# Inverting the first two pairs of chunks side by side, with 14 weight conversions ahead of them: a recurrent attention and two MLPs on one Trainium2 core

## The chip, the core and the metric

The kernel runs on one core of one Trainium2 chip. The core has five engines that each take their own instructions in order: PE (matmuls and, through an identity, transposes), DVE (element by element work), ACT (copies, casts, activations and a DMA queue), POOL (element by element work and a DMA queue) and SP (a DMA queue only). They meet at semaphores. The transfers of all three queues run on 16 DMA engines. The metric is the device time of one execution in microseconds.

## What is computed

Three stages follow each other. First a recurrence over 768 time steps for 4 x 8 = 32 pairs of batch and head, each with a 40 x 40 state:

```python
for t in range(S):                      # B, H, S, D = 4, 8, 768, 40
    y[:, :, t] = np.einsum('bhd,bhde->bhe', rt, state)
    Sa = np.einsum('bhde,bhe->bhd', state, at)
    state_decay = state * wt[:, :, None, :] - np.einsum('bhd,bhe->bhde', Sa, bt)
    state = state_decay + np.einsum('bhd,bhe->bhde', vt, kt)
```

Its output, as x of 3072 tokens by 320, goes through an MLP with 2048 hidden units (`h = x @ w_in`, an ELU, `g @ w_out`), and that through a routed MLP: each token goes to the expert of 8 that its largest logit names (`relu(x @ w1[e]) @ w2[e]`, times the gate). All is in float32; `w_in` and `w_out` come as float64.

## The kernel before

**The recurrence in chunks.** The 768 steps are cut into 24 chunks of 32 (`C`), two chunks make a pair, and there are 12 pairs (`NP`). Four pieces of work serve a pair `p`:

- `lanes(g)`, once for two pairs: products of the decays `w` along the chunk, and `a`, `b`, `k` scaled by them, written to DRAM (`scr_A`, `scr_W`, `scr_BK`). Group 0 runs on DVE at the start, the later ones on POOL.
- `pre(p)`: loads the scaled rows into `tok` tiles, transposes them on PE (L253, PSUM tag "p", one bank), forms the products of a chunk (L288), masks them on DVE into `keep` (L294) and stores the part that has to be inverted in DRAM, as `Td[p]` (L299).
- `inverse(p)`: loads `Td[p]` (64 triangular matrices of 32 x 32) on SP into both halves of a tile (L315) and inverts them on DVE in 31 steps. A step is three instructions: a tensor product into `ut` (L323), an update of one column (L328, with a scalar for each partition) and an addition (L330). The tile `inv` holds input and result. The result goes to DRAM as `Ud[p]` (L334) and from there into the `UT` tiles of the two chunks (L339).
- `chain(c)`, once a chunk: X from v and the state (L398), its product with U (L383 on `X,UT`, evacuated into `pv`, L412 and L414), the state update on DVE (L428, L429), GN (L441), the output `xtok` (L456) and its transposes for the MLP. Chunk c + 1 needs chunk c's state.

**Weights.** `Moe1.weights` turns `w_in` and `w_out` from float64 into two float32r parts, in 40 conversions. One is fetched through ACT's queue into one of three `raw` tiles, goes through an absolute value on ACT (L515), four or five instructions on DVE (L516 to L519, L481) and a copy on ACT; those of `w_out` also have transposes (L556) and small matmuls (L560) on PE. `block(p)` is the first MLP for a pair, 16 hidden tiles each (L609, then L613 to L615, then L623 to L625), and needs the weights and the outputs of both chunks.

**Order.** A scheduler puts the instructions of all engines in order when the program is built. It follows the order in which the code is written, except that pieces in `ahead(tc, g, offset)` come forward by so many places. `tc.issue_after(ins)` queues what a block writes on the engine of `ins` behind `ins`. `weave` takes steps of several generators in turn. At the start `first` (lanes 0, `pre(0)`, `inverse(0)`, lanes 1) is woven with nine conversions, then `pre(1)` with the rest. In the loop over `p` the chain of pair `p`, `inverse(p + 1)`, `pre(p + 2)`, a part of lanes and `block(p - 1)` are woven.

Of the kernel before, what the change touches and what calls it, by code (L numbers as in the profile page):

```python
# [10 lines left out]
F32 = mybir.dt.float32  # L11
# [6 lines left out]
ALU = mybir.AluOpType  # L18
# [20 lines left out]
class Attention:  # L39
# [31 lines left out]
    def setup(self, ident, psum):  # L71
# [52 lines left out]
        self.loaded = self.taken = self.banks = 0  # L124

    def lanes(self, g, eng, eng2=None, room=None):
# [53 lines left out]
        ps = self.psum("p")  # L180
# [39 lines left out]
    def load_tok(self):  # L220
# [3 lines left out]
        kind, i = self.order[self.loaded]  # L224
        t = self.t("tok", self.loaded)
# [82 lines left out]
    def inverse(self, p):  # L308
# [27 lines left out]
        for cc in range(2):  # L336
            for b in range(4):
                h = 32 * cc + 8 * b
                self.returned = self.nc.sync.dma_start(  # L339
                    self.t("UT", 2 * p + cc)[32 * b:32 * b + 32], self.Ud[p][:, h:h + 8, :])  # L340
        yield

# [28 lines left out]
    def chain(self, c, put):  # L371
# [88 lines left out]
        if c + 2 < NCH:  # L460
            self.load_pv(c + 2)
        nc.scalar.copy(xt[:, 320:384], xt[:, 256:320])
# [21 lines left out]
class Moe1:  # L484
# [81 lines left out]
    def begin_x(self, ctx, i):  # L566
        pool = ctx.enter_context(self.tc.tile_pool(name=f"moe1_x{i}", bufs=1))
        self.xH.append(pool.tile([128, 3, 256], F32R, name=f"xH{i}"))
        self.xL.append(pool.tile([128, 3, 256], F32R, name=f"xL{i}"))
# [471 lines left out]
def drain(g):  # L1041
    for _ in g:
        pass
# [31 lines left out]
def body(ctx, tc, r, k, v, w, a, b, w_in, w_out, w_gate, w1, w2, out, capacity=768):  # L1075
# [27 lines left out]
    moe1.begin(st["moe1"], psum)  # L1103
    put = moe1.put_x(ident, psum)
    stage = ExitStack()
    pool = stage.enter_context(tc.tile_pool(name="stage", bufs=1))
# [11 lines left out]
    def start():  # L1118
        lanes = att.lanes(0, nc.vector, room=room)
        for _ in range(25):  # L1120
            next(lanes)
            yield
        pre = att.pre(0)
        drain(lanes)
        yield from pre
        inverse = att.inverse(0)
        next(inverse)
        with tc.issue_after(att.last.ins):
            att.load_pv(0)
            att.load_bkd(0)  # L1130
            att.load_wp(0)
            att.load_pv(1)
        yield
        drain(att.lanes(1, nc.gpsimd))
        yield from inverse
# [15 lines left out]
    weave((first, 20), (behind(att.scaled.ins, some(conv, 9)), 20))  # L1151
    weave((ahead(tc, att.pre(1), 1000), 10), (behind(att.inverted.ins, conv), 40))
    lanes = None
    for p in range(NP + 1):
        gens = []
        if p < NP:
# [3 lines left out]
            if p + 1 < NP:  # L1160
                gens.append((ahead(tc, att.inverse(p + 1), 1500), 20))
# [3 lines left out]
        if p == 1:  # L1165
            stage.close()
            moe1.begin_x(stage, 2)
# [75 lines left out]
```

## Time and profile before

| | |
|---|---|
| time, median of 3 runs | 1213.22 us (1212.05 to 1215.55) |
| time of the profiled execution | 1217.03 us |
| its span, first to last instruction | 1215.3 us |
| PE busy | 1027.2 us (85%) |
| DVE busy | 822.6 us (68%) |
| ACT busy | 599.1 us (49%) |
| POOL busy | 256.1 us (21%) |
| mean granted clock of PE | 0.904 of full speed |

A busy share is an average over stages with different limits; what a change in one stage is worth is read in that stage. Rows give a start in us from the span's beginning, a length in us, the engine and the line in the kernel's code. The profiled execution took 3.8 us more than the median.

### The profile page before, as it was taken

Reading aid. Unit: us, or ns where it says so; the run is one execution under the profiler, and the core shown is the slowest. Engines: PE = TensorE matmul, PEld = TensorE weight load, DVE = VectorE, ACT = ScalarE, POOL = GpSimd, SP = SyncE. Lnnn points to the kernel's source line nnn. Section 1 sums busy time; section 2 is a strip of 40 time slices with the busy share of each in tenths; the row PEclk is TensorE's granted clock in tenths of the full one; section 3 lists DMA queues with packets and bytes.
Section 4 is the critical chain, followed back from the end, with each engine's and each line's share of the span. In section 5 each row is a group of like instructions: output and inputs, shape, how many; then the busy total and the mean of one; then the engine's idle time right before and its main releaser. Section 6 shows DMA issues by size and latency. Waiting matters only on the chain.

```text
span 1215.3 us, 35896 instructions
## 1 busy us (share of the span) xinstructions
PE 1027.2 (85%) x14568; PEld 933.5 (77%) x14568; DVE 822.6 (68%) x2755; ACT 599.1 (49%) x1499; POOL 256.1 (21%) x314
## 2 busy tenths in 40 slices
PE   0454588888988989889999979999998798989995
PEld 0344478777976988779888879888988697979995
DVE  6676798998679576968596949686445456545541
ACT  1432246564654655556556655656655345434420
POOL 5355543410035100400000000000001232323311
PEclk9855669899998989899999989999989999989998
DMA  6887667663356544452616351522131165544210
GB/s 217 205 196 217 188 166 173 194 132 65 62 103 176 104 67 81 106 104 51 108 31 101 58 104 30 91 50 44 27 88 25 39 188 159 164 134 124 82 45 22
DMA packets 294400, 131.27 MB, mean 108 GB/s; under 512 B 261560, under 2 KB 276032, under 8 KB 294224
## 3 DMA queue, kind: packets, MB, share of 16 engines
q1 hardware_dynamic: 276672, 76.39, 32.2%
q0 software_dynamic: 10064, 37.39, 9.7%
q10 hardware_dynamic: 7488, 15.09, 4.1%
q8 instruction: 117, 1.92, 0.7%
q14 instruction: 59, 0.48, 0.1%
HBM read 99.13 MB, written 31.00 MB: 107 GB/s over the span
## 4 chain that ended last, share of the span: by engine, by line
PE 41%; DVE 27%; DMA 19%; ACT 5%; issue 5%; SPq 2%; POOL 1%; ACTq 0%; POOLq 0%; DVEq 0%
PE ps_h L609 8%; PE ps_c L383 4%; DVE inv L328 4%; DVE inv L330 4%; DVE ut L323 3%; DMA out_dram<-ys,ids 3%; DMA inv<-Td 3%; PE ps_o L623 3%; PE ps_o L625 3%; PE ps_o L624 3%; PE ps_c L931 2%; DMA Td<-keep 2%; PE ps_h L931 2%; DMA r<-in_moe_w_dram 2%; DMA Ud<-inv 2%
## 5 line engine op out<-in xcount | busy, mean ns | idle before, releaser
L480 ACT CAST gH<-e 128x256 fp32r<-128x256 f32 x192 | 77.2, 405 | 116.7 <-DVE e L615 102.0
L623 PE MATMUL ps_o<-woH,gH 128*128 128x328 f32 x384 | 129.5, 340 | 5.2 <-ACT gH L480 4.5
L728 POOL DMA_INDIRECT list<-ids,idx x24 | 24.1, 1004 | 498.4 <-DVE idx L724 306.8
L624 PE MATMUL ps_o<-woL,gH 128*128 128x328 f32 x384 | 125.7, 329 | 0.0
L625 PE MATMUL ps_o<-woH,gL 128*128 128x328 f32 x384 | 120.7, 336 | 4.9 <-DVE gL L481 4.8
L615 DVE SCALAR_TENSOR_TENSOR e<-e,ps_h 128x256 f32<-128x256 f32 x184 | 76.2, 415 | 69.0 <-ACT e L614 65.5
L609 PE MATMUL ps_h<-xH,wiH 128*128 128x256 f32 x368 | 113.0, 308 | 10.4 <-DVE e L615 6.6
L323 DVE TENSOR_TENSOR ut<-inv 128x30 f32<-128x30 f32 (+4 forms) x360 | 93.2, 259 | 29.0 <-DMA inv<-Td 28.6
L609 PE MATMUL ps_h<-xL,wiH 128*128 128x256 f32 x368 | 108.6, 295 | 0.0
L609 PE MATMUL ps_h<-xH,wiL 128*128 128x256 f32 x368 | 108.5, 296 | 0.0
L328 DVE SCALAR_TENSOR_TENSOR inv<-inv 128x1 f32<-128x1 f32 (+15 forms) x372 | 101.5, 273 | 0.6
L330 DVE TENSOR_TENSOR inv<-inv,ut 128x30 f32<-128x30 f32 (+4 forms) x360 | 99.7, 277 | 0.2
L481 DVE TENSOR_TENSOR gL<-e,gH 128x256 fp32r<-128x256 f32 x192 | 81.3, 426 | 26.7 <-ACT gH L480 23.3
L253 PE MATMUL ps_p<-ident,tok 128*104 128x128 f32 x288 | 55.0, 320 | 49.4 <-DMA tok<-scr_A 24.8
L613 ACT ACTIVATE e<-ps_h 128x256 f32<-128x256 f32 x184 | 70.3, 384 | 53.4 <-PE ps_h L609 33.9
L609 PEld LDWEIGHTS ps_h<-xH,wiH 128*128 128x128 f32 x368 | 73.7, 201 | 15.0 <-DVE e L615 9.5
L623 PEld LDWEIGHTS ps_o<-woH,gH 128*128 128x128 f32 x384 | 76.8, 200 | 7.7 <-ACT gH L480 5.5
L614 ACT ACTIVATE e<-e 128x256 f32<-128x256 f32 x192 | 79.1, 417 | 4.3
L625 PEld LDWEIGHTS ps_o<-woH,gL 128*128 128x128 f32 x384 | 73.6, 199 | 7.9 <-DVE gL L481 7.2
L253 PEld LDWEIGHTS ps_p<-ident,tok 128*104 128x104 f32 x288 | 35.9, 148 | 56.4 <-issue 25.5
L624 PEld LDWEIGHTS ps_o<-woL,gH 128*128 128x128 f32 x384 | 77.1, 201 | 0.5
L609 PEld LDWEIGHTS ps_h<-xL,wiH 128*128 128x128 f32 x368 | 74.1, 201 | 0.1
(323 smaller groups left out, 2867.5 us busy)
## 6 DMA issues: line engine op xcount, KB each, us to landing
r<-in_moe_w_dram SPq DMA_DIRECT2D x15, 640.0 KB
tok<-scr_BK SPq DMA_DIRECT2D x48, 160.0 KB
BKd<-scr_BK SPq DMA_DIRECT2D x48, 160.0 KB
r<-in_moe_w_dram SPq DMA_DIRECT2D x7, 1024.0 KB
W<-in_w_dram POOLq DMA_DIRECT2D x10, 640.0 KB, 6.3
scr_BK<-lx POOLq DMA_DIRECT2D x10, 640.0 KB, 3.5
inv<-Td SPq DMA_DIRECT2D x24, 256.0 KB
raw<-in_moe_w_out_dram ACTq DMA_DIRECT2D x16, 320.0 KB
```

What stands on the lines that cost most here:

```text
L253: self.nc.tensor.transpose(ps[0:104, 128 * j:128 * j + 128], t[:, 2 * q:2 * q + 2, :].rearrange("p a e -> p (a e)")[:, 0:104], self.ident,)
L323: nc.vector.tensor_tensor(tv, TL[:, j:j + 1, j + 2:32].to_broadcast([128, n, m]), UL[:, 0:n, j:j + 1].to_broadcast([128, n, m]), ALU.mult,)
L328: nc.vector.scalar_tensor_tensor(col, UL[:, 0:n, j], TL[:, j, j + 1:j + 2], col, ALU.mult, ALU.add)
L330: self.inverted = nc.vector.tensor_tensor(UL[:, 0:n, j + 2:32], UL[:, 0:n, j + 2:32], tv, ALU.add)
L480: split.last = nc.scalar.copy(H, x)
L481: return (low or nc.vector).tensor_tensor(L, x, H.bitcast(F32), ALU.subtract)
L609: nc.tensor.matmul(h, l, r, start=i == 0, stop=i == len(seq) - 1)
L614: nc.scalar.activation(e, e, AF.Exp, scale=-1.0)
L615: nc.vector.scalar_tensor_tensor(e, e, -1.0, h, ALU.add, ALU.max)
L623: nc.tensor.matmul(o, gH[:, ts], self.woH[:, f], start=f == 0, stop=False)
L624: nc.tensor.matmul(o, gH[:, ts], self.woL[:, f], start=False, stop=False)
L625: nc.tensor.matmul(o, gL[:, ts], self.woH[:, f], start=False, stop=f == NF - 1)
```

## The change

Pairs 0 and 1 are no longer inverted one after the other. `pre(1)` is written ahead of the inverse, with the priority of `first`. A new `inverses` loads `Td[0]` and `Td[1]` into a tile `twice` of its own and does the 31 steps for both at once: the two tensor instructions of a step now have twice the elements, and the column update, whose scalar differs by pair, is written twice. The results of both pairs are stored, then U is loaded for chunks 0, 1 and 2; as there are three `UT` tiles, that for chunk 3 is loaded in chunk 0's chain, behind its `xtok`. The loop starts with `inverse(2)`, at `p` = 1.

Around it: 14 conversions instead of nine are woven with `first`, and the other 26 are written behind the joint inverse. One load of `tok` rows, ("a", 2), is held until the loads for the inverse and those behind it stand in SP's queue. The transposes of lanes 1 use PSUM tag "o". `stage` (the `raw` and `xf` tiles, later `xH2` and `xL2`) lies on the right side, and the MLP's working tiles are opened when `twice` is given back.

```diff
         self.loaded = self.taken = self.banks = 0
+        self.hold = True
 
...
-        ps = self.psum("p")
+        ps = self.psum("o" if g == 1 else "p")
...
         kind, i = self.order[self.loaded]
+        if self.hold and (kind, i) == ("a", 2):
+            return
...
         for cc in range(2):
-            for b in range(4):
-                h = 32 * cc + 8 * b
-                self.returned = self.nc.sync.dma_start(
-                    self.t("UT", 2 * p + cc)[32 * b:32 * b + 32], self.Ud[p][:, h:h + 8, :])
-        yield
+            self.load_ut(p, cc)
+        yield
+
+    def inverses(self, room):
+
+        nc = self.nc
+        TL = room.rearrange("p (q a b) -> p q a b", q=2, a=32)
+        UL = self.inv[:, 0:1024].rearrange("p (q a b) -> p q a b", q=2, a=16)
+        ut = [self.inv[:, 1024 + 256 * i:1280 + 256 * i] for i in range(2)]
+        nc.vector.memset(self.inv[:, 0:1024], 0.0)
+        for i in range(2):
+            half = slice(64 * i, 64 * i + 64)
+            for q in range(2):
+                self.last = self.nc.sync.dma_start(TL[half, q], self.Td[q])
+                nc.vector.memset(self.inv[half, 512 * q:512 * q + 512][:, i::34], 1.0)
+        yield
+        for j in range(31):
+            n, m = j // 2 + 1, 30 - j
+            if m:
+                tv = ut[j % 2][:, 0:2 * n * m].rearrange("p (q a b) -> p q a b", q=2, a=n)
+                nc.vector.tensor_tensor(
+                    tv, TL[:, :, j:j + 1, j + 2:32].to_broadcast([128, 2, n, m]),
+                    UL[:, :, 0:n, j:j + 1].to_broadcast([128, 2, n, m]), ALU.mult,
+                )
+            for q in range(2):
+                col = UL[:, q, 0:n, j + 1]
+                nc.vector.scalar_tensor_tensor(
+                    col, UL[:, q, 0:n, j], TL[:, q, j, j + 1:j + 2], col, ALU.mult, ALU.add)
+            if m:
+                rest = UL[:, :, 0:n, j + 2:32]
+                self.inverted = nc.vector.tensor_tensor(rest, rest, tv, ALU.add)
+            if j % 2 == 1:
+                yield
+        for p in range(2):
+            for i in range(2):
+                self.nc.sync.dma_start(
+                    self.Ud[p].rearrange("(a i) l t -> i l a t", i=2)[i], UL[64 * i:64 * i + 64, p])
+            for cc in range(2 - p):
+                self.load_ut(p, cc)
+        yield
+
+    def load_ut(self, p, cc):
+        for b in range(4):
+            h = 32 * cc + 8 * b
+            self.returned = self.nc.sync.dma_start(
+                self.t("UT", 2 * p + cc)[32 * b:32 * b + 32], self.Ud[p][:, h:h + 8, :])
...
+        if c == 0:
+            self.load_ut(1, 1)
...
     moe2 = Moe2(tc, nc, w1, w2, out, route, ident)
     moe1.begin_x(st["moe1"], 0)
     moe1.begin_x(st["moe1"], 1)
-    moe1.begin(st["moe1"], psum)
+    moe1.psum = psum
     put = moe1.put_x(ident, psum)
     stage = ExitStack()
-    pool = stage.enter_context(tc.tile_pool(name="stage", bufs=1))
+    pool = stage.enter_context(tc.tile_pool(name="stage", bufs=1, side="right"))
+    beside = ExitStack()
+    twice = beside.enter_context(tc.tile_pool(name="beside", bufs=1)).tile([128, 2048], F32, name="twice")
...
     conv = moe1.weights(pool, route)
         pre = att.pre(0)
         drain(lanes)
         yield from pre
-        inverse = att.inverse(0)
+        yield from att.pre(1)
+        inverse = att.inverses(twice)
         next(inverse)
         with tc.issue_after(att.last.ins):
             att.load_pv(0)
             att.load_bkd(0)
             att.load_wp(0)
             att.load_pv(1)
-        yield
-        drain(att.lanes(1, nc.gpsimd))
+            drain(att.lanes(1, nc.gpsimd))
+            att.hold = False
+            att.load_tok()
+        yield
         yield from inverse
...
 
     with tc.issue_after(att.landed.ins):
         next(conv)
-    weave((first, 20), (behind(att.scaled.ins, some(conv, 9)), 20))
-    weave((ahead(tc, att.pre(1), 1000), 10), (behind(att.inverted.ins, conv), 40))
+    weave((first, 26), (behind(att.scaled.ins, some(conv, 14)), 20))
+    drain(behind(att.inverted.ins, conv))
+    beside.close()
+    moe1.begin(st["moe1"], psum)
     lanes = None
...
             gens.append((ahead(tc, chained(att.chain(2 * p, put), att.chain(2 * p + 1, put)), 2000), 32))
             if p % 2 == 0:
                 lanes = att.lanes(p // 2 + 2, nc.gpsimd) if p // 2 + 2 < NP // 2 else iter(())
-            if p + 1 < NP:
+            if p > 0 and p + 1 < NP:
                 gens.append((ahead(tc, att.inverse(p + 1), 1500), 20))
             if p + 2 < NP:
                 gens.append((ahead(tc, att.pre(p + 2), 1500), 20, 6))
             gens.append((ahead(tc, some(lanes, 14) if p % 2 == 0 else lanes, 500 if p == 0 else 2000), 14))
         if p == 1:
             stage.close()
-            moe1.begin_x(stage, 2)
+            moe1.begin_x(stage, 2, side="right")
```

In the built programs the lines of the changed kernel are numbered otherwise: L294 became L297, L323 to L330 became L360 to L370 for the joint inverse (L326 to L333 for the later ones), L339 became L384, L428 and L429 became L472 and L473, L456 became L500, L516 to L519 became L562 to L565.

On DVE, at the entry of the first inverse. Before, it begins right behind the second mask of pair 0 (`keep`, L294) and the copies of lanes 1 (`WCT`):

```order
L481 TENSOR_TENSOR woL<-x_565,woH 128x320
L294 TENSOR_TENSOR keep<-ps_p,m_tm_131 128x512
L184 COPY WCT_147<-ps_p 40x64
L185 COPY WCT_147<-ps_p 40x64
L481 TENSOR_TENSOR woL<-ps_r,woH 128x8
L323 TENSOR_TENSOR ut_179<-inv 128x30
L328 SCALAR_TENSOR_TENSOR inv<-inv 128x1
L330 TENSOR_TENSOR inv<-inv,ut_179 128x30
```

In the changed kernel the joint inverse begins behind the fourth mask, the second of pair 1, and behind the 14th conversion, whose last instructions stand around that mask:

```order
L565 SCALAR_TENSOR_TENSOR xf<-raw,xf 128x320
L159 MEMSET W_143 128x40
L297 TENSOR_TENSOR keep<-ps_p,m_tm_131 128x512
L527 TENSOR_TENSOR woL<-xf,woH 128x320
L527 TENSOR_TENSOR woL<-ps_r,woH 128x8
L360 TENSOR_TENSOR inv<-twice,inv 128x60
L366 SCALAR_TENSOR_TENSOR inv<-inv,twice 128x1
L370 TENSOR_TENSOR inv<-inv 128x2x30
```

So the inverse moved behind two more masks and five more conversions.

On SP, the queue of loads and stores around the first inverse. Before, the load for pair 0's inverse (`inv<-Td0`) stands behind the second store of `Td0`, and the loads of v, BKd and Wp for chunk 0 follow it; `Td1` comes later:

```order
L299 DMA Td0_107<-keep_166 32x16x32 x2
L315 DMA inv_178<-Td0_107 64x1024 x2
L213 DMA pv0_151<-in_v_dram 32x16x40 x2
L349 DMA BKd0_175<-scr_BK0_101 64x16x40 x2
L354 DMA Wp0_176<-scr_W0_95 32x8x40 x4
L213 DMA pv1_152<-in_v_dram 32x16x40 x2
L239 DMA tok1_150<-scr_BK0_101 64x16x40 x2
L213 DMA tok0_149<-in_r_dram 64x16x40 x2
L299 DMA Td1_108<-keep_166 32x16x32 x2
```

In the changed kernel both stores of `Td1` and the load of it stand ahead of chunk 0's v, BKd and Wp:

```order
L302 DMA Td0_107<-keep_166 32x16x32 x2
L353 DMA twice_231<-Td0_107 64x1024 x2
L242 DMA tok1_150<-scr_BK0_101 64x16x40 x2
L214 DMA tok0_149<-in_r_dram 64x16x40 x2
L302 DMA Td1_108<-keep_166 32x16x32 x4
L353 DMA twice_231<-Td1_108 64x1024 x2
L214 DMA pv0_151<-in_v_dram 32x16x40 x2
L393 DMA BKd0_175<-scr_BK0_101 64x16x40 x2
L398 DMA Wp0_176<-scr_W0_95 32x8x40 x4
```

Chunk 0's loads moved behind pair 1's store and load, and the last rows of pair 1 ahead of all of them.

On DVE again, in chunk 0's state update (`ST`). Before, the first steps of pair 1's inverse stand between its two halves:

```order
L428 TENSOR_TENSOR ST_155<-ps_c,ST_155 40x8x40 x2
L516 SCALAR_TENSOR_TENSOR x_789<-x_789,raw 128x256
L429 TENSOR_TENSOR ST_155<-ST_155,WCT_146 40x8x40 x2
L517 TENSOR_SCALAR raw<-x_789 128x256
L323 TENSOR_TENSOR ut_179<-inv 128x30
L328 SCALAR_TENSOR_TENSOR inv<-inv 128x1
L428 TENSOR_TENSOR ST_155<-ps_c,ST_155 40x8x40 x2
```

In the changed kernel only conversions are mixed in:

```order
L565 SCALAR_TENSOR_TENSOR x_963<-raw,x_963 128x256
L472 TENSOR_TENSOR ST_155<-ps_c,ST_155 40x8x40 x2
L473 TENSOR_TENSOR ST_155<-ST_155,WCT_146 40x8x40
L527 TENSOR_TENSOR wiL<-x_963,wiH 128x256
L473 TENSOR_TENSOR ST_155<-ST_155,WCT_146 40x8x40
L472 TENSOR_TENSOR ST_155<-ps_c,ST_155 40x8x40 x2
```

The inverse's steps are gone from there. Counted over DVE's whole order, 24 of the 40 conversions begin ahead of chunk 1's `xtok` before and 32 in the changed kernel. Ahead of chunk 5's `xtok` stand all 40 in both, with 31 hidden tiles of the first MLP before and 32 in the changed kernel, and the whole inverses of pairs 0 to 3 in both.

## Rows read from the trace of the kernel before

**Rows 1.** Busy time by stretch: stretch, length, engines' busy us, granted clock, DMA share, GB/s.
```profile
core 0: us, PE busy (x) PEld busy (x) DVE busy (x) ACT busy (x) POOL busy (x), PEclk, DMA share, GB/s
60.00:80.00 20.00, 10.05 (x62) 6.97 (x61) 11.15 (x40) 6.72 (x14) 11.14 (x14) 0.50 1.05 233
...
142.56:182.73 40.17, 31.78 (x541) 26.80 (x539) 34.67 (x103) 17.35 (x44) 17.53 (x25) 0.66 0.73 191
182.73:337.39 154.66, 136.44 (x2319) 121.61 (x2315) 130.63 (x446) 89.73 (x248) 30.98 (x35) 0.92 0.55 124
302.34:337.39 35.05, 35.05 (x606) 32.49 (x601) 22.79 (x78) 21.68 (x56) 0.00 (x0) 0.91 0.36 58
405.49:530.05 124.56, 114.59 (x2128) 103.39 (x2127) 94.50 (x361) 71.53 (x182) 15.76 (x13) 0.93 0.47 86
```

**Rows 2.** DVE in order of time, inverse of pair 0: start, length, instruction, idle before.
```profile
70.55 0.19 DVE L323 TENSOR_TENSOR ut<-inv 128x30 f32<-128x30 f32 x1 [5.38 <-DMA inv<-Td]
...
72.74 2.85 DVE L328 SCALAR_TENSOR_TENSOR inv<-inv 128x2 f32<-128x2 f32 x1
...
79.41 0.28 DVE L323 TENSOR_TENSOR ut<-inv 128x120 f32<-128x120 f32 x1
79.60 0.23 DVE L328 SCALAR_TENSOR_TENSOR inv<-inv 128x6 f32<-128x6 f32 x1
79.74 0.28 DVE L330 TENSOR_TENSOR inv<-inv,ut 128x120 f32<-128x120 f32 x1
...
91.05 0.19 DVE L323 TENSOR_TENSOR ut<-inv 128x30 f32<-128x30 f32 x1
...
92.86 0.24 DVE L328 SCALAR_TENSOR_TENSOR inv<-inv 128x16 f32<-128x16 f32 x1
```

**Rows 3.** The chain that ended last: stores and loads of Td, pairs 0 and 1.
```profile
61.49 3.79 DMA Td<-keep
...
65.86 4.66 DMA inv<-Td
...
106.94 8.99 DMA Td<-keep
...
116.50 8.85 DMA inv<-Td
```

**Rows 4.** PE in order of time: pair 1's last product, chunks 0 and 2.
```profile
86.35 0.69 PE L288 MATMUL ps_p<-Abd,BKT 104*64 104x64 f32 x8
...
104.30 0.31 PE L383 MATMUL ps_c<-X,UT 32*32 32x40 f32 x2 [6.87 <-DMA UT<-Ud]
...
191.91 0.79 PE L383 MATMUL ps_c<-pv,keep 32*32 32x40 f32 x64
...
207.70 0.76 PE L383 MATMUL ps_c<-X,UT 32*32 32x40 f32 x60
```

**Rows 5.** DVE in order of time: xtok of chunks 0, 1 and 5.
```profile
142.56 0.48 DVE L456 TENSOR_TENSOR xtok<-ps_c,Wp 128x320 f32<-128x320 f32 x1
...
182.73 0.49 DVE L456 TENSOR_TENSOR xtok<-ps_c,Wp 128x320 f32<-128x320 f32 x1
...
337.39 0.48 DVE L456 TENSOR_TENSOR xtok<-ps_c,Wp 128x320 f32<-128x320 f32 x1
```

**Rows 6.** DVE in order of time, chunk 0: two long waits, in square brackets.
```profile
112.36 0.49 DVE L516 SCALAR_TENSOR_TENSOR x<-x,raw 128x320 f32<-128x320 f32 x1 [3.07 <-ACT x L515]
...
125.45 0.48 DVE L323 TENSOR_TENSOR ut<-inv 128x30 f32<-128x30 f32 x1 [4.88 <-DMA inv<-Td]
```

**Rows 7.** DVE in order of time: the 1st, 9th, 24th and 40th conversion's first instruction.
```profile
22.31 0.42 DVE L516 SCALAR_TENSOR_TENSOR x<-x,raw 128x256 f32<-128x256 f32 x1
...
57.39 0.49 DVE L516 SCALAR_TENSOR_TENSOR x<-x,raw 128x320 f32<-128x320 f32 x1 [0.40 <-ACT x L515]
...
177.85 0.49 DVE L516 SCALAR_TENSOR_TENSOR x<-x,raw 128x320 f32<-128x320 f32 x1 [0.25 <-ACT x L515]
...
276.60 0.48 DVE L516 SCALAR_TENSOR_TENSOR xf<-xf,raw 128x320 f32<-128x320 f32 x1
```

**Rows 8.** Groups by line, PE, chunks 2 to 5 (182.73 to 337.39): count, busy us, mean ns.
```profile
L560 PE MATMUL ps_r<-wg,raw 128*128 128x8 f32 (+1 forms) x48 | 7.7, 269 | 0.3 <-ACT raw L558 0.3
```

More of the change, by code (lines that the diff above doesn't have):

```diff
@@ L564, in weights, with begin_x @@
                 yield
-    def begin_x(self, ctx, i):
-        pool = ctx.enter_context(self.tc.tile_pool(name=f"moe1_x{i}", bufs=1))
+    def begin_x(self, ctx, i, **kw):
+        pool = ctx.enter_context(self.tc.tile_pool(name=f"moe1_x{i}", bufs=1, **kw))
         self.xH.append(pool.tile([128, 3, 256], F32R, name=f"xH{i}"))
```

## The prediction, made before the changed kernel ran

> **What bounds the kernel now.** I read the busy shares by stretch first, then DVE's and PE's instructions in order of time from 20 to 410 us, then the chain that ended last where a transfer stands in it. The reader is to see that no engine is full early on: in 60 to 80 us PE is busy half the time at a granted clock of 0.50, the lower of its two levels, DVE 56%, and only the DMA engines are full (1.05) [rows 1]. The front is a chain of latencies: mask of the products, store and load of Td, the inverse on DVE, store and load of its result, then chunks 0 and 1. Later PE fills up: all 35.05 us of the sixth chunk, and 114.59 of 124.56 us (92%) in chunks 8 to 11 [rows 1]. So the change is worth what it does to the moment at which chunk 5 ends: in both orders all 40 conversions, 31 or 32 hidden tiles of the first MLP and the inverses of pairs 0 to 3 stand ahead of that point on DVE, and behind it the orders run alike. I call the write of xtok a chunk's end: chunk 0 at 142.56, chunk 1 at 182.73, chunk 5 at 337.39 [rows 5].
>
> **The change, step by step, on the clock of the profiled execution.** That one took 1217.03 us, 3.8 above the median of 1213.22; the difference found is carried over to the median.
>
> *The joint inverse starts later.* Before, pair 0's inverse starts at 70.55 [rows 2], behind a store of 3.79 and a load of 4.66 us [rows 3], and pair 1's front work runs under it. Now it needs pair 1's last mask. The product for that one ended on PE at 87.0 (86.35 + 0.69) [rows 4], with a transpose of r ahead of it; 86 for the end of the mask. Then follow an issue, the store, an issue and the load: 0.5 + 3.8 + 0.5 + 4.7 = 9.5 us as for pair 0, or 0.5 + 9.0 + 0.5 + 8.9 = 18.9 as for pair 1 [rows 3]. I take 11, near the lower, because pair 0's crossing came in a slice with full DMA engines and the loads of v, BKd and Wp that stood there now queue behind this one on SP. Start 97 (95 to 105).
>
> A rule speaks against that choice. The Trainium skill, page "DMA: Bandwidth & Descriptors", section "Issuing engines are not separate DMA queues", says that transfers from different engines run on the same 16 DMA engines and interleave: the raw weights of the five conversions moved ahead, 1.4 MB (256 or 320 KB each), would then hold Td back by an estimated 6 us at the slice's 233 GB/s. By it the sum would be 6 us worse; the upper end of 105 covers as much without it.
>
> *Its length.* 120 elements take 0.28 and 30 take 0.19 us: 1.0 ns each. A step is two such tensor operations and a column operation; the first two start 0.19 apart and the next follows after 0.14 (79.41, 79.60, 79.74) [rows 2], so a step with 120 elements is 0.19 + 0.14 + 0.19 = 0.52 us, 0.28 of it fixed. Over 31 steps a pair has 2600 elements in each of the two lines: 31 x 0.28 + 5.2 = 13.9 us, 27.8 for two pairs. Jointly the column operation is issued twice: 31 x (0.28 + 0.14) + 10.4 = 23.4 us. The inverse of pair 0 really ran to 93.1 (92.86 + 0.24) with stretches like the 2.85 us at 72.74 [rows 2], taken while POOL worked on 1280 elements; I leave one in: 26.3. End 123.3. Were there no fixed part, it would be 27.8, 4.4 more.
>
> *The way back.* From the inverse's end to chunk 0's product with U took 11.2 us (93.1 to 104.30) [rows 2, 4]; two more stores are issued ahead of the loads, at the 0.6 us or so that lies between a landing and the next transfer [rows 3]: +1.2. Chunk 0's product at 135.7, **31 us later**.
>
> *Chunk 0* took 38.3 us from there. DVE stood 3.07 us at a conversion's raw weights and 4.88 us at the load for pair 1's inverse, which was queued ahead of the second state update [rows 6]. The second wait is gone with that inverse; of the first, the next raw weights come while U travels. 38.3 - 3.1 - 4.9 = 30.3, and DVE has less mixed in: I take 29 (25 to 36). End 164.7, +22.
>
> *Chunk 1* took 40.2 us, with sixteen inner steps of pair 1's inverse (8.3 us by the step above) and six conversions; now none and eight. A conversion is four DVE instructions of 0.42 to 0.49 us [rows 7] and a shorter one, which overlap, an estimated 1.75 us: 40.2 - 8.3 + 3.5 = 35.4, and a little less since raw weights wait less for DVE: 34 (31 to 42). End 198.7, **+16**, with 32 conversions done instead of 24, and U of pair 1 at hand.
>
> *Chunks 2 to 5* took 154.7 us with PE busy 136.4 of them [rows 1], at 88%. Chunk 2's X was begun at 191.91, but 60 of the 64 matmuls of its product with U ran only at 207.70, as U of pair 1 was landing [rows 4]; that wait of some 12 us goes, and eight conversions (14 us of DVE, which is busy 130.6 of 154.7 us) as well. PE's work shrinks little: eight conversions of w_out took 7.7 us in L560 alone [rows 8], three of them move ahead, an estimated 4.5 us with their transposes: 132. Between all of PE's time (132) and the later 92% (143) I take 97%, 136 us. End of chunk 5: 334.7 against 337.4, **-2.7 us**.
>
> *What I count as nothing.* PSUM tag "o" for lanes(1) has no other user before the block after chunk 1; without that cover it would wait for an evacuation of half a microsecond, as xtok's [rows 5]. The held load ("a", 2) is first used by pre(2), in chunk 1's time; late, it would shift pair 2's inverse, which has chunks 2 and 3 as cover. Tiles that move sides take no instruction; e and gH fall into the room of `twice`, last read by the joint inverse 70 us before. UT for chunk 3 is loaded after chunk 0's end, two chunks ahead. The one place to watch is SP: v, BKd and Wp of chunk 0 stand behind the load that waits for Td of pair 1. The copy of chunk 0's X stands inside the joint inverse on DVE; if v lands late, DVE stops there for up to the 4 to 9 us of a transfer [rows 3].
>
> Sum: +31.4 - 9.3 - 6.2 - 18.7 = about -3 us. **Forecast 1210 us.**
>
> **Rivals.**
>
> *Slower: the conversions set the pace.* DVE takes its instructions in order, and 15 conversions, each behind its own load and with three raw buffers, stand between the joint inverse's end and chunk 1's end. The first nine came 4.4 us apart (22.31 to 57.39), the 24th to 40th 6.2 apart (177.85 to 276.60) [rows 7]. My end of chunk 1 needs (198.7 - 123.3) / 15 = 5.0. At 6.2 it is 216.3 and chunk 5 ends at 352.3: +15; the block, less hampered by conversions, may give back a third: 1223 us. It decides from about 5.2 us a conversion on. For it: DMA engines 73% busy through chunk 1 of before [rows 1]. Against it: the 6.2 was measured with two inverses and block work on the same DVE.
>
> *No gain from chunks 2 to 5.* PE stays at 92%: 143 us, chunk 5 at 341.7, +4, 1217 us. For it: that is what chunks 8 to 11 show. Against it: the sixth chunk's 100% with DVE at 65%.
>
> *More gain.* The front at its lower ends: 95 + 26.3 + 12.4 + 25 + 31 + 136 = 325.7, -12, 1201 us; with PE never waiting (132), 1197. I price it at 1200. For it: chunks 0 and 1 lose both other users of DVE at once.
>
> *The fusion saves nothing* because the cost goes with the elements: +4.4, 1214 us, as the second rival.
>
> **How the numbers follow.** Forecast 0.45, with a range of its own of 1204 to 1216; conversions 0.24; no gain, or a fusion without saving, 0.11; more gain 0.20. A difference of under 0.3% (3.6 us) is about what a measurement of this kernel can't tell from no change. Faster: 0.20 of the forecast's 0.45, 0.20, and 0.01 of the third: 0.41. Same: 0.21 + 0.07 = 0.28. Slower: 0.04 + 0.24 + 0.03 = 0.31. Range 1196 to 1224: outside lie a front bound by the 18.9 us of transfers on top of slow conversions, and a part of the case with more gain, together under 0.2.
>
> **What would show it.** Joint inverse from 97 to 123; chunk 0's product with U near 136; ends of chunk 0 near 165 and chunk 1 near 199; chunk 2's product in one piece behind its X; chunk 5 near 335. It is wrong if the joint inverse starts past 103, if chunk 1 ends past 206 or before 190, or if chunks 2 to 5 take under 130 or over 142 us. If chunk 5 moves and the end doesn't follow, the later stages had slack that I did not see.

## The result and the profile after

The changed kernel took 1231.18 us (median of 1223.13, 1233.03, 1229.34 and 1234.45), the kernel before 1213.53 on the same chip: a ratio of 1.0115, 95% interval 1.0073 to 1.0158. It is slower, where 1210 was forecast, and outside the range of 1196 to 1224. Ratios, here and below, leave out executions that took over 1.5% more than the fastest of the same kernel. The profiled execution is the fastest of the four (span 1221.3 us), and that of the kernel before was above its median (span 1215.3 us), so the two traces show 6.0 us of the loss and the medians 17.7; what is said of a moment is on the clock of the trace.

DVE's rows in order of time, the joint inverse alone (start, us, engine, line, operation, tiles, shapes, idle before and its releaser), answer to [rows 2]:

```profile
93.32 0.22 DVE L360 TENSOR_TENSOR inv<-twice,inv 128x60 f32<-128x60 f32 x1 [5.14 <-DMA twice<-Td]
...
99.19 0.33 DVE L442 COPY X<-ps_c 128x160 f32<-128x160 f32 x1 [2.38 <-PE ps_c L427]
...
106.73 2.98 DVE L366 SCALAR_TENSOR_TENSOR inv<-inv,twice 128x6 f32<-128x6 f32 x2
...
129.53 3.01 DVE L366 SCALAR_TENSOR_TENSOR inv<-inv,twice 128x15 f32<-128x15 f32 x2
...
132.71 0.40 DVE L366 SCALAR_TENSOR_TENSOR inv<-inv,twice 128x15 f32<-128x15 f32 x2
...
134.75 0.27 DVE L366 SCALAR_TENSOR_TENSOR inv<-inv,twice 128x16 f32<-128x16 f32 x2
```

It runs from 93.32 to 135.02 (134.75 and the 0.27 us of that row), 41.7 us. A pair of column operations of 15 elements took 0.40 us at 132.71; another such pair took 3.01, and one of 6 elements 2.98. POOL's rows in order of time show what ran beside them:

```profile
106.62 2.93 POOL L175 TENSOR_TENSOR lx<-lx,W 128x1280 f32<-128x1280 f32 x1
...
129.45 2.89 POOL L197 TENSOR_TENSOR lx<-lx,W 128x1280 f32<-128x1280 f32 x1
```

The chain of waits of the changed kernel through the front (start, us, what) shows the crossings of Td (pair 0's first, then pair 1's store), the late v, the way back, and three loads of raw weights in chunk 0:

```profile
58.78 6.63 DMA Td<-keep
...
65.97 5.88 DMA twice<-Td
...
84.78 3.27 DMA Td<-keep
88.20 0.48 SPq L353
...
89.99 7.83 DMA pv<-in_v_dram
97.86 1.30 PE ps_c L427 x60
99.19 0.33 DVE X L442
...
135.56 3.93 DMA Ud<-inv
139.50 6.08 DMA UT<-Ud
...
150.47 7.08 DMA raw<-in_moe_w_in_dram
...
163.53 5.21 DMA raw<-in_moe_w_in_dram
...
171.58 5.85 DMA raw<-in_moe_w_out_dram
```

PE's row of chunk 0's product with U in order of time (104.30 in [rows 4]):

```profile
145.62 1.99 PE L427 MATMUL ps_c<-X,UT 32*32 32x40 f32 x64 [5.04 <-DMA UT<-Ud]
```

In chunk 0 DVE stood at three conversions whose raw weights had not come, for the time in square brackets:

```profile
158.09 0.97 DVE L562 SCALAR_TENSOR_TENSOR x<-x,raw 128x256 f32<-128x256 f32 x1 [5.23 <-ACT x L561]
...
169.28 0.42 DVE L562 SCALAR_TENSOR_TENSOR x<-x,raw 128x256 f32<-128x256 f32 x1 [1.83 <-ACT x L561]
...
177.43 0.43 DVE L562 SCALAR_TENSOR_TENSOR xf<-xf,raw 128x256 f32<-128x256 f32 x1 [4.61 <-ACT xf L561]
```

DVE's rows at the ends of chunks 0, 1 and 5, which answer to [rows 5]:

```profile
181.03 0.49 DVE L500 TENSOR_TENSOR xtok<-ps_c,Wp 128x320 f32<-128x320 f32 x1
...
214.54 0.48 DVE L500 TENSOR_TENSOR xtok<-ps_c,Wp 128x320 f32<-128x320 f32 x1
...
361.52 0.49 DVE L500 TENSOR_TENSOR xtok<-ps_c,Wp 128x320 f32<-128x320 f32 x1 [1.16 <-DMA tok<-in_r_dram]
```

The product came 41.3 us later than before, chunk 0's end 38.5, chunk 1's 31.8, chunk 5's 24.1. The busy times by stretch (length, then busy us of PE, PEld, DVE, ACT and POOL with instructions, granted clock, DMA share, GB/s) in stretches of the changed kernel: beside the inverse, chunk 1, chunks 2 to 5, and of these chunk 2 alone and chunks 3 to 5:

```profile
100.00:140.00 40.00, 4.29 (x25) 3.17 (x23) 38.32 (x117) 1.33 (x4) 23.47 (x27) 0.50 0.47 124
181.03:214.54 33.51, 26.98 (x561) 24.39 (x559) 22.67 (x57) 19.38 (x53) 0.00 (x0) 0.84 0.51 112
214.54:361.52 146.98, 128.05 (x2288) 115.92 (x2288) 118.04 (x397) 82.20 (x222) 30.84 (x35) 0.94 0.51 112
214.54:257.88 43.34, 36.72 (x575) 32.58 (x575) 37.70 (x106) 26.15 (x72) 12.76 (x12) 0.88 0.62 161
257.88:361.52 103.64, 91.33 (x1715) 83.34 (x1714) 80.34 (x292) 56.04 (x151) 18.08 (x24) 0.97 0.46 91
```

The kernel before in the same view: the first of these stretches, the time between X and the product with U in chunk 2 ([rows 4]), chunk 2, and chunks 3 to 5:

```profile
100.00:140.00 40.00, 20.99 (x273) 18.31 (x277) 27.30 (x81) 9.86 (x26) 20.97 (x25) 0.50 0.64 183
191.91:207.70 15.79, 12.45 (x164) 11.16 (x163) 12.48 (x32) 8.96 (x26) 7.04 (x7) 0.89 0.89 210
182.73:238.56 55.83, 47.50 (x653) 42.91 (x650) 48.54 (x130) 31.86 (x92) 24.29 (x25) 0.91 0.68 177
238.56:337.39 98.83, 88.94 (x1669) 78.70 (x1667) 82.09 (x318) 57.87 (x157) 6.69 (x10) 0.93 0.47 94
```

From 100 to 140 us PE worked 4.29 us where it had worked 20.99: DVE was full with the inverse until 135, and no chunk could go on. Chunks 2 to 5 took 147.0 us with PE busy 87% of them, no more than before. PE stood idle 18.9 us (146.98 less 128.05), against 18.2 before (154.66 less 136.44 [rows 1]). The two longest sums of its waits in that stretch (line, releaser, us in total, times, longest):

```profile
PE ps_h L655 <- DVE e L661: 11.6, 4, 3.8
PE ps_p L256 <- DMA tok<-scr_A: 2.0, 1, 2.0
```

Chunk 2's wait for U of pair 1 is gone, as forecast, and chunk 2 took 43.34 us instead of 55.83. But that wait had not been PE's: of the 15.79 us between X and the product before, PE worked 12.45, on hidden tiles. By chunk 2's end 8 hidden tiles were through DVE instead of 12; the others now stand in chunks 3 to 5, which took 103.64 us instead of 98.83, and PE waited 11.6 us there and in chunk 2 for DVE to empty the PSUM tiles of hidden tiles.

### The profile page after: what moved, and what is told of

It reads as the page before. It is cut to its first block, busy times and chain, and to the rows that moved or that the text cites. A ratio compares the mean times of both kernels' runs of the same rounds, so it can differ in the third digit from the quotient of the medians.

```text
span 1221.3 us, 35821 instructions
## 1 busy us (share of the span) xinstructions
PE 1004.1 (82%) x14568; PEld 917.4 (75%) x14568; DVE 817.1 (67%) x2694; ACT 599.2 (49%) x1499; POOL 258.3 (21%) x314
## 4 chain that ended last, share of the span: by engine, by line
PE 38%; DVE 27%; DMA 20%; ACT 6%; issue 4%; SPq 3%; POOL 1%; ACTq 0%; POOLq 0%; DVEq 0%
PE ps_h L655 7%; PE ps_c L427 4%; DVE inv L333 4%; DVE ut L326 3%; DVE inv L331 3%; DMA Td<-keep 3%; DMA inv<-Td 3%; PE ps_c L977 3%; PE ps_h L977 3%; PE ps_o L669 2%; PE ps_o L671 2%; PE ps_o L670 2%; DMA xs<-rows,ids 2%; DVE e L661 2%; DVE gL L527 2%
## 5 line engine op out<-in xcount | busy, mean ns | idle before, releaser
L326 DVE TENSOR_TENSOR ut<-inv 128x120 f32<-128x120 f32 (+4 forms) x300 | 79.1, 264 | 26.2 <-DMA inv<-Td 26.0
L333 DVE TENSOR_TENSOR inv<-inv,ut 128x120 f32<-128x120 f32 (+4 forms) x300 | 82.7, 276 | 0.2
L331 DVE SCALAR_TENSOR_TENSOR inv<-inv 128x1 f32<-128x1 f32 (+15 forms) x310 | 79.7, 257 | 0.6
L655 PEld LDWEIGHTS ps_h<-xH,wiL 128*128 128x128 f32 x368 | 72.3, 197 | 0.1
```

The costliest lines, as they stand in the source:

```text
L326: nc.vector.tensor_tensor(tv, TL[:, j:j + 1, j + 2:32].to_broadcast([128, n, m]), UL[:, 0:n, j:j + 1].to_broadcast([128, n, m]), ALU.mult,)
L331: nc.vector.scalar_tensor_tensor(col, UL[:, 0:n, j], TL[:, j, j + 1:j + 2], col, ALU.mult, ALU.add)
L333: self.inverted = nc.vector.tensor_tensor(UL[:, 0:n, j + 2:32], UL[:, 0:n, j + 2:32], tv, ALU.add)
L655: nc.tensor.matmul(h, l, r, start=i == 0, stop=i == len(seq) - 1)
```

## Experiments

All ratios are to the kernel before on the same chip, with 95% intervals.

**The change once more, and its two halves alone.** The changed kernel again:

> The changed kernel once more, beside the others on one chip. Every theory expects what was measured: 1223 to 1235 us, about 1.2% over the kernel before; the joint inverse from about 93 to 135, chunk 0's end near 181, chunk 1's near 215, chunk 5's near 362 on the trace's clock.

1.0109 (1.0057 to 1.0162). The joint inverse with the old number of conversions:

```diff
-    weave((first, 26), (behind(att.scaled.ins, some(conv, 14)), 20))
+    weave((first, 26), (behind(att.scaled.ins, some(conv, 9)), 20))
```

> The joint inverse with 9 conversions in front of it instead of 14, so 20 instead of 15 stand between its end and chunk 1's end. Theory W (the loss is the wait for pair 1: chunk 0 starts 35 to 40 us later, and the conversions only fill the wait): the joint inverse starts a few us sooner (87 to 93), chunk 0's product comes within 6 us of 145.6, and the end is 1226 to 1238 us. Rival C (the conversions on DVE and their raw weights set the pace of chunks 0 and 1): at the 5.3 us of the changed kernel five more of them put chunk 1's end at 230 to 240 instead of 214.5, and the end is 1240 to 1255 us.

1.0128 (1.0082 to 1.0175), 1233.56 us. The inverse ran from 87.83 to 122.17, the product came at 128.07 and chunk 0 ended at 160.43, 21 us sooner than in the changed kernel, which theory W had not expected. Chunk 1 ended at 193.91, not at 230 to 240, so rival C's numbers fail. But the edit did not make rival C's case: only 13 conversions, not 20, began between the inverse's end and chunk 1's end, 5.5 us apart, where it is 15 and 5.3 in the changed kernel, and the rest came later (the 40th at 287.69 instead of 262.30). Whether conversions pace chunks 0 and 1 stays open by this run. The lead was worth nothing at the end. The conversions alone:

```diff
-    weave((first, 20), (behind(att.scaled.ins, some(conv, 9)), 20))
+    weave((first, 20), (behind(att.scaled.ins, some(conv, 14)), 20))
```

> The kernel before with 14 conversions instead of 9 in front, and no joint inverse. Theory W: the inverse of pair 0 still starts by 75 and ends by 98, chunk 0's product with U comes at 105 to 112, and the end is 1206 to 1217 us, that is no loss. Rival C (five more conversions ahead of the inverse delay Td and its mask): chunk 0's product past 115 and 1220 us or more.

0.9906 (0.9874 to 0.9938), 1207.21 us: faster than both kernels, with chunk 0's product at 108.24. Once more, in another session but on the same chip, not on another as planned:

> The kernel before with 14 conversions in front, once more and on another chip, since 12 and 18 were no faster. If its gain is of its order, which is fixed in the program, it is there again: a ratio of 0.986 to 0.995. If it was of the chip or the hour: 0.997 or more.

0.9896 (0.9860 to 0.9933). So the loss stands with the joint inverse, and 14 conversions alone gain about 1%. With 12 and with 18 in the same line:

> The kernel before with 12 conversions in front instead of 9. Theory F (conversions in front use time in which DVE and PE wait, so each is worth about the same, 11 us for five): 1207 to 1211 us on the scale on which the kernel before has 1213.5, a ratio of 0.993 to 0.996. Rival S (the gain of 14 was one draw of the order that the scheduler makes anew for each kernel): no gain or a loss, a ratio from 0.998 up.

> The kernel before with 18 conversions in front. Theory F: a ratio of 0.980 to 0.987, unless their raw weights begin to hold Td back: then chunk 0's product comes past 112 and the ratio is 0.988 to 0.996. Rival S: 0.998 or more with chunk 0's product by 112.

1.0038 (1.0001 to 1.0076) and 1.0067 (1.0029 to 1.0104). Theory F fails for 12. With 18, the inverse of pair 0 ran from 77.01 to 114.48 and the product came at 130.11, past the 112 of theory F's reserve, but the ratio lies above the 0.988 to 0.996 that it gave for that; rival S had the product by 112. With 12 the product came at 104.07 and the ratio still is just over 1. So the front alone doesn't order 12 and 14. The order behind it, which the scheduler makes anew for each kernel, is the candidate that the kernels with a held order below take up, for 14.

**GpSimd beside the joint inverse.** Two writes of one element on DVE, queued behind the joint inverse, hold back the loads of the third group's lanes and so POOL's work:

```diff
+            if g == 2:
+                with self.tc.issue_after(self.inverted.ins):
+                    nc.vector.memset(W[:, 1, 0:1], 1.0)
+                    nc.vector.memset(la[:, 0, 0:1], 1.0)
```

> The changed kernel, with the loads of pair group 2's lanes and so GpSimd's work on them held back until the joint inverse has ended. Theory L (GpSimd's work on wide tiles stretches the joint inverse's DVE instructions, some 10 to 13 of its 41.7 us): the joint inverse takes 28 to 32 us, its instructions of 2.9 us are gone, chunk 0's product comes at 132 to 136 and the end is 6 to 12 us under the changed kernel's. Rival P (the stretch only moved conversions and waits about, and raw weights pace the time after it): the inverse is shorter but chunk 1 still ends past 210 and the end is within 4 us of the changed kernel's. Rival N (GpSimd isn't the cause): the inverse still takes 38 us or more.

1.0199 (1.0153 to 1.0245). DVE's first and last row of the inverse, and the ends of chunks 0 and 1:

```profile
93.70 0.22 DVE L364 TENSOR_TENSOR inv<-twice,inv 128x60 f32<-128x60 f32 x1 [5.28 <-DMA twice<-Td]
...
119.28 0.26 DVE L370 SCALAR_TENSOR_TENSOR inv<-inv,twice 128x16 f32<-128x16 f32 x2
...
158.95 0.48 DVE L504 TENSOR_TENSOR xtok<-ps_c,Wp 128x320 f32<-128x320 f32 x1
...
200.87 0.49 DVE L504 TENSOR_TENSOR xtok<-ps_c,Wp 128x320 f32<-128x320 f32 x1 [0.59 <-PE ps_c L431]
```

The inverse takes 25.8 us, so theory L is right about its length: of the 15.9 us less, 2.1 are the copy of X, which now waited 0.24 us, and up to 13.8 went with POOL's work. It is wrong about the worth, and rival P, which had chunk 1 past 210, fails too. The same kernel's busy times in chunk 1:

```profile
158.95:200.87 41.92, 27.92 (x495) 24.40 (x496) 28.65 (x59) 18.16 (x47) 19.96 (x26) 0.59 0.74 202
```

Chunk 1 took 41.9 us instead of 33.5, with PE granted 0.59 instead of 0.84 and the DMA engines 74% busy instead of 51%, as POOL's lanes now ran there; chunk 5 ended at 355.19, and the ratio is 0.009 worse than the changed kernel's.

**Without the wait for pair 1.** The inverses taken apart, pair 1's in the room of the joint tile:

```diff
-        yield from att.pre(1)
-        inverse = att.inverses(twice)
+        inverse = att.inverse(0)
         next(inverse)
...
         yield from inverse
+        yield from att.pre(1)
+        yield from att.inverse(1, twice)
```

> The changed kernel with the joint inverse taken apart: pair 0 is inverted from its own Td as soon as that has landed, in the buffers of before, and pair 1 behind it in the room of the joint tile; pair 1's front work, the 14 conversions and all else stay as changed. Theory W (the loss is the wait of pair 0 for pair 1): the inverse of pair 0 starts by 78 and ends by 106, chunk 0's product with U comes by 118 and the end is 1203 to 1216 us, the same as or under the kernel before. Rival M (what costs is pair 1's work pulled ahead of chunk 0 and the order that the scheduler makes of it, joint or not): 1222 us or more with chunk 0 no more than 10 us earlier than in the changed kernel, or with its lead lost by chunk 5.

1.0109 (1.0045 to 1.0172), so theory W's time fails. Pair 0's inverse started at 77.49, the product came at 106.08, chunk 0 ended at 134.90 and chunk 5 at 336.21, 1.2 us sooner than in the kernel before, but then with 23 hidden tiles done instead of 31. The later 26 conversions stood behind pair 1's inverse, and between 84 and 164 us only three began on DVE (from 149.55 on). With them behind pair 0's:

```diff
         yield from inverse
+        att.alone = att.inverted
...
-    drain(behind(att.inverted.ins, conv))
+    drain(behind(att.alone.ins, conv))
```

> The joint inverse taken apart as in the run before with free order, but with the 26 later conversions right behind pair 0's inverse, where the kernel before has them, instead of behind pair 1's: there only three conversions ran between 91 and 165 us. It is the changed kernel without the wait for pair 1, and with its 14 conversions, pair 1's early front work and the free order. Theory W (the wait for pair 1 is the loss; that run failed by the place of the conversions): chunk 0 ends by 150, the 30th hidden tile comes by 330 and the ratio is 0.988 to 1.002. Rival G (it isn't the wait: pair 1's front work and inverse pulled ahead cost as much): 1.006 or more with chunk 0 by 150.

1.0151 (1.0102 to 1.0200). DVE's rows at the ends of chunks 0 and 2:

```profile
145.39 0.48 DVE L504 TENSOR_TENSOR xtok<-ps_c,Wp 128x320 f32<-128x320 f32 x1
...
251.63 0.48 DVE L504 TENSOR_TENSOR xtok<-ps_c,Wp 128x320 f32<-128x320 f32 x1
```

The busy times in the stretch behind chunk 2:

```profile
251.63:300.00 48.37, 35.54 (x610) 29.25 (x609) 27.72 (x112) 18.32 (x48) 21.29 (x28) 0.61 0.80 180
```

Theory W fails and rival G holds. Here the 40th conversion began at 228.58 us, and PE did all 16 hidden tiles of the first block ahead of chunk 2's end; then it had none left until chunk 3 had ended (283.41), worked 35.54 of 48.37 us, and its granted clock fell to 0.61. Of chunk 0's lead of 36 us over the changed kernel 6.3 were left at chunk 2. The last way to take the wait away, the joint inverse fed with pair 0's Td twice, which leaves out the inverse of pair 1, so that the data from chunk 2 on are others:

```diff
-                self.last = self.nc.sync.dma_start(TL[half, q], self.Td[q])
+                self.last = self.nc.sync.dma_start(TL[half, q], self.Td[0])
```

> The joint inverse reads the Td of pair 0 twice, so it doesn't wait for pair 1 but is as long. It leaves out the true inverse of pair 1: chunks 2 and 3 get that of pair 0, the attention and the routing behind it are other data, and so only the ends of chunks and hidden tiles are read, up to chunk 23's end, not the end of the kernel. Theory W: the joint inverse starts by 78, and the whole front moves with it: chunk 0's product at 120 to 132, the 30th hidden tile by 342 instead of 351, chunk 23's end at 878 to 888 instead of 893 to 905. Rival L (the length of the joint inverse beside GpSimd's work is the loss, not the wait): it still takes 38 us or more, chunk 0's product comes past 130 and the 30th hidden tile past 346.

The first step stood at 72.88, the rest from 79.75 to 124.47, longer than with the wait (a conversion queued among the steps waited 4.51 us for its weights); product at 131.90, chunk 0's end at 154.84, the 30th hidden tile at 323.59 instead of 351.22, chunk 23's end at 881.66 instead of 892.71. Theory W's numbers hold but for the start, and so does rival L's on the length. The whole took 1.0102 (1.0033 to 1.0171), with these other data.

**Front and order taken apart.** In the kernels before and after, DVE's rows between the ends of chunks 5 and 21, compared chunk by chunk without buffer numbers, agree in part only: 51 to 78% of a chunk's instructions stand in the same order in both. So the program was made to keep an order: what it writes from the second turn of its main loop on is the same 13554 instructions in both, and a table holds for each engine in which order they stand in one of them.

```diff
+    late = list(nc.cur_bb.bb.instructions)[traced:]
...
+                tc.add_manual_dep(
+                    late[at], before.name,
+                    mybir.DependencyInfo(mybir.DependencyClass.NoSync, mybir.DependencyReason.DATA),
```

An edge of this kind is meant to set the place in the queue and to add no wait. No run holds a kernel's own order on its own front, so what the edges cost isn't measured by itself.

> The changed front, and behind it the order of the kernel before: all 13554 instructions that the program writes from the second turn of its main loop on (pair 2's inverse, chunks 2 to 23, all blocks of the first MLP but for what stands ahead of them, the sparse layer) are held, engine by engine, in the order in which they stand in the kernel before; from chunk 5 on the two kernels' rows are the same. Theory R (the change's 1.1% comes from the new order that the scheduler made of everything behind it, not from the front): a ratio to the kernel before of 0.997 to 1.004. Theory W (it comes from chunk 0's start, 40 us later): 1.008 to 1.016, with the 60th hidden tile 15 to 25 us later than in the kernel before. A ratio between them would share it out.

> The front of the kernel before, and behind it the order of the changed kernel, held in the same way. Theory R: 1.008 to 1.014, the changed kernel's loss without its front. Theory W: 0.996 to 1.003. Rival O (each late order suits only the front it was made for): both this and the kernel with the two exchanged are over 1.008.

> The kernel before with 14 conversions in front, and behind it the order of the kernel before, held in the same way. Theory R: the gain of 0.9% is gone, 0.996 to 1.004, as 12 and 18 conversions gained nothing. Theory W, by which the front's lead is kept: 0.987 to 0.994.

> The changed front, and behind it the order of the kernel before with 14 conversions, the fastest one so far, held in the same way. Theory R: 0.987 to 0.995, the first version with the joint inverse that beats the kernel before. Theory W: 1.005 or more.

| front | order of before | order of changed | order with 14 |
|---|---|---|---|
| before | 1 | 1.0031 (0.9998 to 1.0064) | |
| changed | 1.0204 (1.0147 to 1.0260) | 1.0109 (1.0057 to 1.0162) | 1.0106 (1.0059 to 1.0153) |
| 14 conversions | 1.0077 (1.0046 to 1.0108) | | 0.9906 (0.9874 to 0.9938) |

Theory R falls for the changed kernel: with the order of before its front costs 2.0%, with its own order 0.8% (1.0109 against 1.0031), and with the order of 14 conversions 2.0% more than the front with 14. In the first column it costs more than theory W had. There the later rows are those of before, and so the delay can be followed. Chunk 5's end on DVE, with the changed front and the order of before:

```profile
364.14 0.48 DVE L504 TENSOR_TENSOR xtok<-ps_c,Wp 128x320 f32<-128x320 f32 x1
```

The same kernel's busy times from there to the end:

```profile
364.14:1241.10 876.96, 800.01 (x11079) 737.92 (x11077) 559.96 (x1930) 453.24 (x1118) 136.22 (x139) 0.95 0.40 87
```

The kernel before, from its chunk 5's end ([rows 5]) to its end:

```profile
337.39:1215.30 877.91, 800.68 (x11079) 737.63 (x11077) 561.83 (x1930) 453.58 (x1118) 135.48 (x139) 0.95 0.39 87
```

The same 11079 matmuls took 876.96 and 877.91 us, so the edges add nothing there. A delay of 26.8 us at chunk 5 is one of 25.8 at the end. The changed kernel's own order gives back half of it (1.0109 instead of 1.0204). For the 14 conversions theory R holds in that their gain is there with their own order only; with the order of before there even is a loss (1.0077), which it had not expected. An order made for another front costs clearly in these two cases (some 0.9 and 1.7%). In the other two it doesn't: 1.0031 (0.9998 to 1.0064) isn't clear of 1, and the changed front runs as long with the order of 14 as with its own.

**The front's steps with the order of the changed kernel held behind them**, the edits being those above:

> The changed kernel with GpSimd's lanes of the third group held back until the joint inverse has ended, and behind the front the order of the changed kernel held, so that no new order stands between the edit and the end. Theory L (the 16 us by which the joint inverse ran past 26 us beside GpSimd's work are part of the loss): chunk 0 ends by 162, and as a delay of chunk 5 went to the end in full, the ratio to the kernel before falls from 1.011 to 0.997 to 1.004. Rival G (the held-back lanes and raw weights take the time back in chunks 0 to 3, so the front has another limit): chunk 5 ends within 6 us of the 361 to 365 of the changed kernel and the ratio is 1.008 to 1.016.

> The joint inverse with 9 conversions in front instead of 14, the order of the changed kernel held behind the front. If the 14 conversions in front pay for part of the wait, this is the same or slower than the changed kernel: 1.010 to 1.020. If they hold the joint inverse back (chunk 0 ended 20 us sooner with 9) and that matters, it is 0.998 to 1.006.

> The joint inverse taken apart (pair 0 inverted as soon as its Td lands, pair 1 behind it), the order of the changed kernel held behind the front. Theory W (the wait for pair 1 is the loss): chunk 0 ends near 135 and the ratio is 0.994 to 1.004. Rival G (the conversions behind the two inverses are the limit: the 40th at 288 instead of 260): chunk 5 ends past 355 in spite of chunk 0's lead of 45 us and the ratio is 1.008 or more.

> The joint inverse that reads the Td of pair 0 twice and so doesn't wait for pair 1 (chunks 2 and 3 get the inverse of pair 0, the data behind them is another, and the times are read up to the last hidden tile), the order of the changed kernel held behind the front. Theory W: chunk 0 ends by 158, chunk 5 by 348 instead of 361 to 365, and the last hidden tile comes at 940 to 952 instead of 959 to 975. Rival G: chunk 5 within 6 us of the changed kernel's.

| edit | chunk 0 ends | chunk 2 | chunk 5 | ratio |
|---|---|---|---|---|
| POOL held back | 162.10 | 252.31 | 356.69 | 1.0107 (1.0058 to 1.0156) |
| 9 conversions | 164.33 | 254.56 | 364.50 | 1.0153 (1.0100 to 1.0206) |
| taken apart | 138.02 | 256.82 | 366.00 | 1.0138 (1.0085 to 1.0191) |
| pair 0's Td twice | 157.08 | 264.72 | 361.43 | 1.0145 (1.0084 to 1.0207) |

Rival G three times, and with nine conversions the first of its two cases: of leads of 17 to 43 us at chunk 0 at most 5.6 are left at chunk 2, which ended at 257.88 in the changed kernel. With the free order it was otherwise: of leads of 21 to 46 us the five kernels (POOL held back, nine conversions, the two taken apart, pair 0's Td twice) still had 6 to 33 at chunk 2 and 6 to 25 at chunk 5 (two of them with four and nine hidden tiles fewer done), and lost them behind it.

## Why the prediction was wrong

Two of the prediction's signs of being wrong came: chunk 1 ended past 206, and chunks 2 to 5 took over 142 us.

**The joint inverse starts later: right.** 93.32 against 97, and a little under the range. Td of pair 1 took 8.9 us from the last mask's end (84.4) to that start, for 11. The Trainium skill's rule ("DMA: Bandwidth & Descriptors", "Issuing engines are not separate DMA queues") had been weighed at an estimated 6 us more; pair 1's store shows none of it, with 3.27 us against 3.79 in [rows 3]. Pair 0's crossing fits it: a store of 6.63 and a load of 5.88 us, where the kernel before had 3.79 and 4.66. The joint inverse did not wait for that one.

**Its length: the first step that failed**, 41.7 us for 26.3. The arithmetic was good: 23.4 without a stretch, and with POOL held back it takes 25.8, some 2 of which are the copy of X, three conversion instructions and a memset among the steps. What failed is the term for POOL's work: one stretch of 2.9 us was counted, and POOL was busy 23.47 of the 40 us from 100 on. The warning stood in [rows 2]: the inverse of pair 0 took 22.5 us where the sum had 13.9. The Trainium skill ("SBUF — State Buffer", "SBUF: two separate sides") says that VectorE, reading two inputs from SBUF, and GpSimd take one shared port pair, locked for a whole instruction; the rows of 2.98 and 2.93 us agree. The copy of X, named as a risk, cost 2.38.

**The way back** was 10.6 us for 12.4, and the product 9.9 later than forecast (145.62 for 135.7; -3.7 + 15.4 - 1.8).

**Chunk 0: the second step that failed**, 35.4 us for 29. The prediction took the wait for raw weights out, as the next ones would come while U travels. Three came, and those behind them did not: DVE stood 5.23, 1.83 and 4.61 us at the rows shown, 11.7 us instead of 3.07, and three loads of raw weights, 18.1 us, stand on the chain that ended last. **Chunk 1** took 33.5 us for 34.

**Chunks 2 to 5: the third step that failed**, 147.0 us for 136. Chunk 2's wait for U was counted as PE's, but PE had filled it with hidden tiles, so that its going moved work and took no idle time away: 18.9 us idle for 18.2. What the stretch gained, 7.7 us, is PE's work getting less (128.05 us for 136.44, where the sum had 132). PE stayed at 87%, not 97%. This was the second rival's mechanism (PE doesn't get fuller), and 4 us more than its 143. The four errors, 9.9 + 6.4 - 0.5 + 11.0, make 26.8 us: +24.1 at chunk 5 for -2.7.

**Behind chunk 5** the prediction took the orders to be alike. They are not, but the premise below it, that a delay there reaches the end, is shown with the order of before held behind the changed front (26.8 us, 25.8 at the end). The changed kernel's own order gave back some 1%: of 24.1 us at chunk 5 the medians keep 17.7 at the end.

**The first rival** came near chunk 1's end (216.3, measured 214.54), in part by luck: the inverse ended 11.7 us later than the rival had it. Its mechanism is there, in chunk 0's waits for raw weights. As the prediction counted, 15 conversions began in the 79.5 us between the inverse's end and chunk 1's end, 5.3 apart: just past the 5.2 from which it decides, and short of its 6.2.

What stays open is the share of each step in the front. Taking away the wait, the stretch or five conversions made chunk 0 17 to 46 us earlier and the end no earlier, with a free order (1.0102 to 1.0199) and with a held one (1.0107 to 1.0153). In both kinds two things change at once, the front and how well the order fits it. That chunk 2's end doesn't follow chunk 0's is shown with the order held; that a lead of 6 to 25 us at chunk 5 is lost behind it is shown with the free order, but not by what. That PE runs out of hidden tiles of the first block is shown for one of these kernels only.

## What to carry over

Where a scheduler lays out the rows when the program is built, an edit in front changes the order of everything behind it, and here that moved the end by up to 1.7% with the front alike (14 conversions, own order or that of before): hold the later order to see what an edit itself does, and test an edit at two or three neighbouring sizes. A step that is early is not yet worth anything at the end: here neither chunk 0's lead nor, with a new order, chunk 5's came out there. Before a wait of one piece of work is counted as an engine's idle time, look at what the engine did in it: here PE worked 12.45 of 15.79 us. Before two things are fused, see what ran in the gap that the fusion removes, and what will now run beside the longer piece.

## What was not expected

GpSimd beside DVE cost up to 13.8 us on an inverse of 25.8, over half more. Running the same program again on a chip scatters more than the first three runs had shown: the kernel before ran from 1209.10 to 1228.73 us in one session, so that single profiles tell of places in the front, and only the ratios tell of the end.
